# Order of VectorE's work within a slot, and the share of dense groups per slot, in an infini-attention and gated-GLU kernel

## The chip, the cores and the metric

The kernel runs on one core of a Trainium2 chip. The time is the device time of one execution in microseconds; the profile's span runs from the first to the last instruction of the program within it. Five engines work side by side, each through its own queue in order: TensorE (PE; its weight loads are PEld), VectorE (DVE), ScalarE (ACT), GpSimd (POOL) and SyncE (SP), which here issues most DMAs.

## What is computed

Part A is a layer norm, three projections, and attention in 32 heads of 20 over 4 segments of 512 rows: causal softmax attention inside a segment, and a read of a memory `M`, `z` that the earlier segments left, mixed by a gate per head. Part B is a gated GLU on the same normalised input, 640 to 1536 and back. The result is `x + A * silu(B)`.

```python
xn = _layernorm(x)                                   # [1, 2048, 640], bf16
for s in range(4):                                   # segments
    p = softmax(q_s @ k_s.T * scale + causal)        # per head
    a_dot = p @ v_s
    a_mem = (phi(q_s) @ M) / (phi(q_s) @ z + 1e-6)   # phi(t) = t + 1 if t > 0 else exp(t)
    o = g * a_mem + (1 - g) * a_dot
    M, z = M + phi(k_s).T @ v_s, z + phi(k_s).sum()
out = x + (o @ wo) * silu((sigmoid(xn @ w_gate) * (xn @ w_up)) @ w_down)
```

## The kernel before

**Slots.** The main loop (L666 to L717) goes through 4 segments of 20 slots. A slot handles one unit of a pair of head groups: `scores` (L495) multiplies keys by queries for four heads into `Sps`, one PSUM tile of four banks, ScalarE takes the exponential of all of it into `pt` (L506), and GpSimd zeroes what lies above the diagonal (L509). One slot later `weigh` (L513) multiplies `pt` by the values into `Aps` (L526), one PSUM tile with a single buffer. Five units make a pair; after the units 2 and 4 of a pair the accumulated `Aps` of a head group is complete, and VectorE does the division (L532 to L535: reciprocal, gate, product into `od`). As units are weighed one slot later, divisions fall into slots 3 and 5, 8 and 10, 13 and 15, 18 and 20 of a segment's count, and the slot after each begins a new `Aps` tile.

**What fills a slot.** Beside scores and weighting there are two kinds of work. The dense groups of the GLU wait in a list, `bulk`: `gate` (L408, matmuls into `gp`, tanh `tg` on ScalarE), `up` (L418, matmuls into `up`, then VectorE's gating product `hT`, L426) and `down` (L429, twelve matmuls into `yp`, tanh `t` on ScalarE, VectorE's product `aa`, L440). Everything else stands in a heap, `tasks`, with a due time in slots and a cost in us of TensorE time (L620 to L656): projections of the next segment (`k_chunk`, `q_chunk`, `v_tile`: `psk`, `psq`, `psv`), the bound `q_bound` (`cps`), the memory's update (`dm`) and read (`am`), the output projection (`o_proj`: `sp`), and work without matmuls: layer-norm statistics (`ln_stats`, L217 to L219) and normalisation (`ln_norm`, L234), the features (`phi`, L347: minimum and sum on VectorE, exponential of `mn` on ScalarE at L355, maximum on VectorE at L359), reductions (`k_max`), and the DMAs that store, relay and transpose. A task may put a follow-up into the heap with `later`.

**How a slot is filled.** `fill` (L682) runs tasks that are due, and dense groups as long as a budget is owed, first up to 0.45 of the slot with 45% of the budget, then, after `weigh`, up to its end. The budget is worked out anew in each slot, so that slots rich in other work get fewer dense groups; and while dense groups are left, each slot gets more until `FLOOR` = 1.2 is reached (L712). Each engine's instructions stand in its queue in just the order in which these functions issue them (`manual_schedule`, L95).

**PSUM.** Of eight banks `Sps` has four, `Aps` one, and all other matmuls share three buffers of the pool `ps_d`, tag `d`. A buffer is free again when ScalarE or VectorE has read it; the pool hands out one that is free in its own plan.

**Start.** `startup` (L552) does segment 0's projections and the relays of queries and keys through DRAM (`Qs`, `Ks`, `Cs` into `QT`, `KT`), loads the GLU's weights in pieces (`load_glu`), normalises segment 1 and runs the first seven dense groups. SP issues its DMAs in the order of the code: `load_glu(1, 0)` (L593) stands ahead of `c_in(0, (0,))` (L594), which loads `QT` from `Cs`.

Of the kernel before, what the change touches and what calls it, by code (L numbers as in the profile page):

```python
# [53 lines left out]
FLOOR = 1.2  # L54
# [5 lines left out]
def kernel(  # L60
# [168 lines left out]
    def ln_norm(n, p, i):  # L229
# [8 lines left out]
        if n == 0:  # L238
            pT = ps_d.tile([P, DC, P], BF, name="pT", tag="d")
# [23 lines left out]
    def k_chunk(n, c):  # L263
# [4 lines left out]
        ps = ps_d.tile([P, L], F32, name="psk", tag="d")  # L268
# [26 lines left out]
    def q_chunk(n, c):  # L295
# [4 lines left out]
        ps = ps_d.tile([P, L], F32, name="psq", tag="d")  # L300
# [9 lines left out]
    def q_bound(n):  # L310
        s = st[n]
        ps = ps_d.tile([P, L], F32, name="cps", tag="d")
# [24 lines left out]
    def v_tile(n, j, half):  # L337
        s = st[n]
        ps = ps_d.tile([P, HB], F32, name="psv", tag="d")
# [27 lines left out]
    def m_update(n, cs):  # L367
        s = st[n]
        dm = ps_d.tile([P, len(cs), HW * VW], F32, name="dm", tag="d")
# [17 lines left out]
    def mem_read(n, j, b):  # L387
# [3 lines left out]
        am = ps_d.tile([P, 16, VW], F32, name="am", tag="d")  # L391
# [16 lines left out]
    def gate(n, f):  # L408
        s = st[n]
        gp = ps_d.tile([P, L], F32, name="gp", tag="d")  # L410
# [7 lines left out]
    def up(n, f):  # L418
        s = st[n]
        ps = ps_d.tile([P, L], F32, name="up", tag="d")  # L420
# [5 lines left out]
        nc.vector.scalar_tensor_tensor(out=h[:], in0=s["tg"][:], scalar=1.0, in1=ps[:], op0=ALU.add, op1=ALU.mult)  # L426
        s.setdefault("hT", []).append(h)

    def down(n, j, half):  # L429
        s = st[n]  # L430
        if half == 0:
            s[f"aa{j}"] = fpool.tile([P, D], BF, name="aa", bufs=4)
        hs = slice(half * HB, (half + 1) * HB)
        yp = ps_d.tile([P, HB], F32, name="yp", tag="d")
        for f in range(FC):
# [4 lines left out]
        nc.vector.scalar_tensor_tensor(out=s[f"aa{j}"][:, hs], in0=t2[:], scalar=1.0, in1=yp[:],  # L440
                                       op0=ALU.add, op1=ALU.mult)
# [18 lines left out]
    def o_last(n):  # L460
        po = ps_d.tile([P, 4, P], BF, name="po", tag="d")
# [12 lines left out]
    def o_proj(n, j, half):  # L474
# [4 lines left out]
        sp = ps_d.tile([P, HB], F32, name="sp", tag="d")  # L479
# [67 lines left out]
    def warm(count):  # L547
        ps = ps_d.tile([P, L], F32, name="wps", tag="d")
# [3 lines left out]
    def startup():  # L552
# [24 lines left out]
        for c in range(DC):  # L577
# [15 lines left out]
        load_glu(1, 0)  # L593
# [10 lines left out]
        take(1)  # L604
        ln_norm(1, 1, 0)
        take(1)
        ln_norm(1, 1, 1)
        take(2)
# [49 lines left out]
    def run_task():  # L658
        time, _, cost, fn, a = heapq.heappop(tasks)
        clock[0] = max(clock[0], time)  # L660
        fn(*a)
        return cost

    owed = 0.0
    due, held = [], []
    for n in range(NSEG):  # L666
# [4 lines left out]
        keep = 4 if n >= NSEG - 2 else 0  # L671
# [95 lines left out]
```

## Time and profile before

| | |
|---|---|
| median of 3 runs | 353.14 us (349.23, 353.14, 353.32) |
| profiled execution | 352.11 us, its span 350.3 us |
| mean granted clock of TensorE | 0.987 |
| first score matmul (slot 0) | 34.0 us |
| last slot begins (slot 79) | 330.9 us |
| TensorE, VectorE, ScalarE, GpSimd busy | 330.3, 216.0, 234.2, 110.7 us |

How to read the profile's lines: `L436 PE MATMUL yp<-Wd,hT 128*128 128x320 bf16 x384` is line 436 of the kernel, engine, operation, what it writes and reads, shapes and count. In a timeline a line begins with its start and its length in us, and merges equal instructions that follow each other; what stands in brackets is the idle time of that engine just before, and what ended it. In the list of waits the numbers are us in total, times, and the longest. In the table by stage each engine has its busy time and its instructions; behind them stand the granted clock, the share of DMA and GB/s. A matmul's record is longer than the distance to the next one, since matmuls are pipelined.

### The profile page before, as it was taken

The page shows a single profiled execution, that of the slowest core. Times are in us where ns is not written, and L with a number is a line of the kernel's source. Part 1 is how long each engine was busy: PE and PEld are TensorE (multiplying, and loading weights), DVE is VectorE, ACT ScalarE, POOL GpSimd, SP SyncE. Part 2 cuts the span into 40 slices and gives each one's busy share as a digit, 9 for nine tenths or more (in the row PEclk, how much of TensorE's full clock was granted, in tenths as well). Part 3 has the DMA queues.
Part 4 walks back from the last instruction along what each step waited for, and adds up shares of the span by engine and source line. Part 5 has one row for each costly group of instructions (what it writes and reads, how often), then busy time and mean ns, then how long its engine had stood idle before and what let it go on. Part 6 is the DMA issues. An engine that isn't in the chain of part 4 may idle for free.

```text
span 350.3 us, 8363 instructions
## 1 busy us (share of the span) xinstructions
PE 330.3 (94%) x3359; PEld 188.9 (54%) x3402; DVE 216.0 (62%) x541; ACT 234.2 (67%) x258; POOL 110.7 (32%) x157
## 2 busy tenths in 40 slices
PE   8998899998969999999987999999999999999995
PEld 7543355545645466554554446555446755544673
DVE  5364374468975456669759556766585688533445
ACT  3652689868694677657777566666778877776730
POOL 6644223222153222323225132231323323223214
PEclk9999999999998999999999899999999999999998
DMA  7947775564721621034740261104231341210032
GB/s 226 353 162 225 140 198 113 177 196 115 193 76 22 112 77 39 19 103 103 176 127 17 52 110 49 37 34 137 84 97 42 39 113 40 75 40 2 2 60 75
DMA packets 54725, 35.53 MB, mean 101 GB/s; under 512 B 28576, under 2 KB 54688, under 8 KB 54688
## 3 DMA queue, kind: packets, MB, share of 16 engines
q1 hardware_dynamic: 52480, 32.23, 35.5%
q10 hardware_dynamic: 2208, 2.79, 2.5%
q8 instruction: 26, 0.43, 0.5%
q14 instruction: 11, 0.09, 0.1%
HBM read 20.19 MB, written 8.39 MB: 82 GB/s over the span
## 4 chain that ended last, share of the span: by engine, by line
PE 73%; DVE 9%; ACT 8%; DMA 4%; issue 3%; SPq 1%; POOL 0%; ACTq 0%; DVEq 0%; POOLq 0%
PE gp L413 13%; PE up L423 13%; PE yp L436 10%; PE Aps L526 8%; PE sp L481 6%; PE Sps L501 5%; PE psv L341 5%; PE psk L270 5%; ACT pt L506 5%; PE psq L302 5%; DMA pkt<-k 2%; PE wps L550 2%; DMA xnT<-xn 1%; PE am L395 1%; ACT mn L355 1%
## 5 line engine op out<-in xcount | busy, mean ns | idle before, releaser
L506 ACT ACTIVATE pt<-Sps 128x2048 bf16<-128x2048 f32 x80 | 150.2, 1877 | 26.4 <-PE Sps L501 22.2
L509 POOL TENSOR_SCALAR_AFFINE_SELECT pt<-pt 128x1024 bf16<-128x1024 bf16 (+1 forms) x80 | 75.9, 948 | 210.2 <-ACT pt L506 210.2
L423 PE MATMUL up<-xnT,Wu 128*128 128x512 bf16 x230 | 59.1, 379 | 2.3 <-DVE hT L426 1.5
L436 PE MATMUL yp<-Wd,hT 128*128 128x320 bf16 x384 | 60.0, 309 | 0.0
L413 PE MATMUL gp<-xnT,Wg 128*128 128x512 bf16 x219 | 58.0, 379 | 1.4 <-issue 0.3
L526 PEld LDWEIGHTS <-pt 128*128 128x128 bf16 x1280 | 42.9, 96 | 22.7 <-DVE od L535 11.5
L426 DVE SCALAR_TENSOR_TENSOR hT<-tg,up 128x512 bf16<-128x512 bf16 x48 | 32.7, 682 | 32.7 <-PE up L423 30.3
L526 PE MATMUL Aps<-va,pt 128*128 128x21 bf16 x1280 | 44.8, 173 | 8.5 <-DVE od L535 7.2
L416 ACT ACTIVATE tg<-gp 128x512 bf16<-128x512 f32 x48 | 28.6, 597 | 26.7 <-PE gp L413 21.1
L436 PEld LDWEIGHTS <-hT 128*128 128x128 bf16 x384 | 36.3, 100 | 16.5 <-issue 2.6
L440 DVE SCALAR_TENSOR_TENSOR aa<-t,yp 128x320 bf16<-128x320 bf16 x32 | 15.6, 487 | 30.7 <-ACT t L439 30.6
L501 PE MATMUL Sps<-QT,KT 24*128 24x128 bf16 (+3 forms) x512 | 32.6, 302 | 1.4 <-DMA QT<-Cs 1.1
L423 PEld LDWEIGHTS <-Wu 128*128 128x128 bf16 x240 | 20.5, 97 | 24.9 <-issue 6.1
L413 PEld LDWEIGHTS <-Wg 128*128 128x128 bf16 x240 | 20.8, 97 | 23.7 <-issue 4.3
L439 ACT ACTIVATE t<-yp 128x320 bf16<-128x320 f32 x32 | 13.9, 436 | 19.9 <-PE yp L436 19.9
L341 PE MATMUL psv<-Wv,xnT 128*128 128x320 bf16 x160 | 26.5, 299 | 0.2
L481 PE MATMUL sp<-Wo,oT 128*128 128x320 bf16 x160 | 25.9, 299 | 0.0
L483 DVE SCALAR_TENSOR_TENSOR aa<-aa,sp 128x320 bf16<-128x320 bf16 x32 | 15.5, 486 | 16.1 <-PE sp L481 16.1
L270 PE MATMUL psk<-xnT,Wk 128*128 128x512 bf16 x95 | 23.8, 380 | 0.2
L302 PE MATMUL psq<-xnT,Wq 128*128 128x512 bf16 x93 | 23.5, 379 | 0.4 <-issue 0.2
L355 ACT ACTIVATE mn<-mn 128x512 bf16<-128x512 bf16 x30 | 19.0, 632 | 5.9 <-DVE mn L351 5.9
L501 PEld LDWEIGHTS <-KT 24*128 24x128 bf16 x512 | 9.5, 92 | 24.0 <-issue 22.6
(73 smaller groups left out, 328.6 us busy)
## 6 DMA issues: line engine op xcount, KB each, us to landing
KT<-Ks SPq DMA_DIRECT2D x32, 80.0 KB
QT<-Qs SPq DMA_DIRECT2D x32, 80.0 KB
xr<-in_A_x_dram SPq DMA_DIRECT2D x15, 160.0 KB
out_dram<-xr SPq DMA_DIRECT2D x15, 160.0 KB
xt<-in_A_x_dram SPq DMA_DIRECT2D x6, 320.0 KB
Wg<-in_B_w_gate_dram SPq DMA_DIRECT2D x3, 640.0 KB
Wu<-in_B_w_up_dram SPq DMA_DIRECT2D x3, 640.0 KB
Wd<-in_B_w_down_dram ACTq DMA_DIRECT2D x1, 1920.0 KB
```

Of the source, the lines that this page charges most:

```text
L270: nc.tensor.matmul(ps[:], lhsT=W["k"][:, k, c * P:(c + 1) * P], rhs=s["xnT"][:, k, :], start=(k == 0), stop=(k == DC - 1))
L302: nc.tensor.matmul(ps[:], lhsT=W["q"][:, k, c * P:(c + 1) * P], rhs=s["xnT"][:, k, :], start=(k == 0), stop=(k == DC - 1))
L341: nc.tensor.matmul(ps[:], lhsT=s["xnT"][:, k, j * P:(j + 1) * P], rhs=W["v"][:, k, half * HB:(half + 1) * HB], start=(k == 0), stop=(k == ...
L413: nc.tensor.matmul(gp[:], lhsT=Wg[f // 4][:, k, fo:fo + P], rhs=s["xnT"][:, k, :], start=(k == 0), stop=(k == DC - 1))
L423: nc.tensor.matmul(ps[:], lhsT=Wu[f // 4][:, k, fo:fo + P], rhs=s["xnT"][:, k, :], start=(k == 0), stop=(k == DC - 1))
L426: nc.vector.scalar_tensor_tensor(out=h[:], in0=s["tg"][:], scalar=1.0, in1=ps[:], op0=ALU.add, op1=ALU.mult)
L436: nc.tensor.matmul(yp[:], lhsT=s["hT"][f][:, j * P:(j + 1) * P], rhs=W["d"][:, f, hs], start=(f == 0), stop=(f == FC - 1))
L481: nc.tensor.matmul(sp[:], lhsT=s["oT"][:, j, c, :], rhs=W["o"][:, c, hs], start=(c == 0), stop=(c == DC - 1))
L501: nc.tensor.matmul(Sps[:, r, c0:c0 + ncol], lhsT=kt[32 * r:32 * r + KR, gi, kb * P:(kb + 1) * P], rhs=qt[32 * r:32 * r + KR, gi, kb * P:L] ...
L506: nc.scalar.activation(pt[:], Sps[:], ACT.Exp, scale=SCALE)
L509: nc.gpsimd.affine_select(out=diag, in_=diag, compare_op=ALU.is_ge, fill=0.0, base=0, pattern=[[0, 4], [0, cnt], [1, P]], channel_multipli ...
L526: nc.tensor.matmul(A[:, qb, r, :], lhsT=pt[:, r, off:off + P], rhs=V[4 * (n % 2) + kb][:, 4 * g + r, :], start=first, stop=True, skip_grou ...
```

## The change

Five things are changed.

1. Tasks with a cost of at most 0.1 (statistics, normalisation, features, reductions, follow-ups, DMAs) go into a second heap, `soft`. The first half of a slot runs only `tasks`, the second half both, in order of due time.
2. VectorE's products of `up` and `down` are put off when they come up in a slot's first half: `empty` keeps them in `pending` until `weigh` has issued its matmuls and the division, or until the third next tile of the pool is taken (`dtile`). `down` puts out all but the last before it goes on.
3. The dense groups' share is worked out once per segment (`level`, `fixed`); a running sum `given` is compared with a running `goal`, of which 45% of a slot's share comes ahead of `weigh`. `FLOOR` is gone.
4. In the startup `load_glu(1, 0)` moves up behind the first store of `Qs`, and the normalisations of segment 1's last two row blocks move out of the startup, into the heap with due times 1.67 and 1.92.
5. `run_task` sets the clock that follow-ups count from to the task's own due time; at the end `drain` empties both heaps.

All tiles of the pool `ps_d` are taken through `dtile`; of these replacements one is shown.

```diff
@@ -51,7 +51,7 @@
 NU = len(UNITS)
 NSLOT = NG // 2 * NU
 WARM = 40
-FLOOR = 1.2
+FIRST = 0.45
 PASS = [0.41, 0.41, 0.41, 0.2, 0.61]
 R = NSLOT / 24
 
@@ -95,13 +95,32 @@
     ctx.enter_context(tc.manual_schedule(engines={ENG.PE, ENG.Activation, ENG.DVE, ENG.Pool, ENG.SP}))
 
 
-    tasks = []
+    tasks, soft = [], []
     count = [0]
     clock = [0.0]
+    pending = []
 
     def at(time, cost, fn, *a):
         count[0] += 1
-        heapq.heappush(tasks, (time, count[0], cost, fn, a))
+        heapq.heappush(tasks if cost > 0.1 else soft, (time, count[0], cost, fn, a))
+
+    seq = [0]
+    delay = [False]
+
+    def flush(keep=0):
+        while len(pending) > keep:
+            pending.pop(0)[1]()
+
+    def dtile(shape, dtype, name):
+        seq[0] += 1
+        while pending and pending[0][0] <= seq[0] - 3:
+            pending.pop(0)[1]()
+        return ps_d.tile(shape, dtype, name=name, tag="d")
+
+    def empty(fn):
+        pending.append((seq[0], fn))
+        if not delay[0]:
+            flush()
 
     def later(lag, fn, *a):
         at(clock[0] + lag * R, 0.0, fn, *a)
@@ -236,7 +255,7 @@
         j = 2 * p + i
         dst = s["xnT"][:, :, j * P:(j + 1) * P]
         if n == 0:
-            pT = ps_d.tile([P, DC, P], BF, name="pT", tag="d")
+            pT = dtile([P, DC, P], BF, "pT")
             for c in range(DC):
                 nc.tensor.transpose(pT[:, c, :], xn[:, c * P:(c + 1) * P], ident[:])
             nc.scalar.copy(dst, pT[:])
...
@@ -417,28 +436,34 @@
 
     def up(n, f):
         s = st[n]
-        ps = ps_d.tile([P, L], F32, name="up", tag="d")
+        ps = dtile([P, L], F32, "up")
         fo = (f % 4) * P
         for k in range(DC):
             nc.tensor.matmul(ps[:], lhsT=Wu[f // 4][:, k, fo:fo + P], rhs=s["xnT"][:, k, :],
                              start=(k == 0), stop=(k == DC - 1))
         h = gpool.tile([P, L], BF, name="hT", bufs=FC)
-        nc.vector.scalar_tensor_tensor(out=h[:], in0=s["tg"][:], scalar=1.0, in1=ps[:], op0=ALU.add, op1=ALU.mult)
+        tg = s["tg"]
+        empty(lambda: nc.vector.scalar_tensor_tensor(out=h[:], in0=tg[:], scalar=1.0, in1=ps[:],
+                                                     op0=ALU.add, op1=ALU.mult))
         s.setdefault("hT", []).append(h)
 
     def down(n, j, half):
         s = st[n]
         if half == 0:
             s[f"aa{j}"] = fpool.tile([P, D], BF, name="aa", bufs=4)
+            if j == 0:
+                flush()
         hs = slice(half * HB, (half + 1) * HB)
-        yp = ps_d.tile([P, HB], F32, name="yp", tag="d")
+        flush(1)
+        yp = dtile([P, HB], F32, "yp")
         for f in range(FC):
             nc.tensor.matmul(yp[:], lhsT=s["hT"][f][:, j * P:(j + 1) * P], rhs=W["d"][:, f, hs],
                              start=(f == 0), stop=(f == FC - 1))
         t2 = fpool.tile([P, HB], BF, name="t2")
         nc.scalar.activation(t2[:], yp[:], ACT.Tanh, scale=0.25)
-        nc.vector.scalar_tensor_tensor(out=s[f"aa{j}"][:, hs], in0=t2[:], scalar=1.0, in1=yp[:],
-                                       op0=ALU.add, op1=ALU.mult)
+        aa = s[f"aa{j}"]
+        empty(lambda: nc.vector.scalar_tensor_tensor(out=aa[:, hs], in0=t2[:], scalar=1.0, in1=yp[:],
+                                                     op0=ALU.add, op1=ALU.mult))
 
 
     def o_add(n, j, c0, c1):
...
@@ -581,6 +606,7 @@
                 relay(0, 0, Ks, KT)
             elif c == 2:
                 stage_out(0, 0, Qs, QT, "q5")
+                load_glu(1, 0)
             if c < 2:
                 ln_stats(1, 0, c, c + 1)
         make_bd()
@@ -590,7 +616,6 @@
         relay(0, 0, Qs, QT)
         q_bound(0)
         stage_out(0, 1, Qs, QT, "q5")
-        load_glu(1, 0)
         c_in(0, (0,))
         load_glu(1, 1)
         ln_stats(1, 1, 0, 1)
@@ -601,11 +626,9 @@
         ln_norm(1, 0, 1)
         take(1)
         ln_stats(1, 1, 1, 2)
-        take(1)
-        ln_norm(1, 1, 0)
-        take(1)
-        ln_norm(1, 1, 1)
-        take(2)
+        take(4)
+        at(R * 2.0, 0.0, ln_norm, 1, 1, 0)
+        at(R * 2.3, 0.0, ln_norm, 1, 1, 1)
         load_glu(2, 0)
         load_glu(2, 1)
         relay(0, 1, Ks, KT)
@@ -655,13 +678,17 @@
         at(NSLOT * NSEG - 8 + 0.5 * j, 0.0, xr_load, NSEG - 1, j)
         at(NSLOT * NSEG - 0.9 + 0.2 * j, 0.0, o_ready, NSEG - 1, j, DC - 1)
 
-    def run_task():
-        time, _, cost, fn, a = heapq.heappop(tasks)
-        clock[0] = max(clock[0], time)
+    def run_task(heap):
+        time, _, cost, fn, a = heapq.heappop(heap)
+        clock[0] = time
         fn(*a)
         return cost
 
-    owed = 0.0
+    def drain():
+        flush()
+        while tasks or soft:
+            run_task(min((h for h in (tasks, soft) if h), key=lambda h: h[0][:2]))
+
     due, held = [], []
     for n in range(NSEG):
         st[n]["od"] = opool.tile([P, 4, D], BF, name="od")
@@ -669,51 +696,47 @@
             bulk += [(1.09, fn, (n, f)) for f in range(FC) for fn in (gate, up)]
         bulk += [(1.64, down, (n, j, h)) for j in range(4) for h in range(2)]
         keep = 4 if n >= NSEG - 2 else 0
+
+        left = sum(b[0] for b in bulk[:len(bulk) - keep])
+        fixed = [PASS[i % NU] + sum(t[2] for t in tasks if i <= t[0] - NSLOT * n < i + 1) for i in range(NSLOT)]
+        level = min(fixed)
+        while sum(max(level - f, 0.0) for f in fixed) < left:
+            level += 0.01
+        given, goal = 0.0, 0.0
+
+        def fill(until, heaps):
+            nonlocal given
+            while True:
+                ready = [h for h in heaps if h and h[0][0] < until]
+                if ready:
+                    run_task(min(ready, key=lambda h: h[0][:2]))
+                if len(bulk) > keep and given + 0.5 * bulk[0][0] <= goal:
+                    cost, fn, a = bulk.pop(0)
+                    given += cost
+                    fn(*a)
+                elif not ready:
+                    break
+
         for slot in range(NSLOT):
             pair, u = divmod(slot, NU)
             now = NSLOT * n + slot
-
-            def more():
-                nonlocal owed
-                cost, fn, a = bulk.pop(0)
-                owed -= cost
-                fn(*a)
-
-            def fill(until, share):
-                nonlocal owed
-                owed += budget * share
-                while True:
-                    if tasks and tasks[0][0] < until:
-                        owed -= run_task()
-                        if not (len(bulk) > keep and owed >= 0.5 * bulk[0][0]):
-                            continue
-                    if len(bulk) > keep and owed >= 0.5 * bulk[0][0]:
-                        more()
-                    elif not (tasks and tasks[0][0] < until):
-                        break
-
-            left = sum(b[0] for b in bulk[:max(len(bulk) - keep, 0)])
-            fixed = [PASS[i % NU] + sum(t[2] for t in tasks if now + i - slot <= t[0] < now + i - slot + 1)
-                     for i in range(slot, NSLOT)]
-            level = min(fixed)
-            while sum(max(level - f, 0.0) for f in fixed) < left:
-                level += 0.01
-            budget = max(level, fixed[0])
-            owed = -PASS[u]
+            share = max(level - fixed[slot], 0.0)
             pt = scores(n, pair, u)
-            fill(now + 0.45, 0.45)
+            delay[0] = True
+            goal += FIRST * share
+            fill(now + 0.45, (tasks,))
             for w in due:
                 weigh(*w)
+            delay[0] = False
+            flush()
             due, held = held, []
             due.append((n, pair, u, UNITS[u][0][0], pt))
             if u == 2:
                 held.append((n, pair, u, 1, pt))
-            fill(now + 1.0, 0.55)
-            while len(bulk) > keep and budget - owed - PASS[u] < FLOOR:
-                more()
+            goal += (1.0 - FIRST) * share
+            fill(now + 1.0, (tasks, soft))
         while len(bulk) > keep:
             cost, fn, a = bulk.pop(0)
-            owed -= cost
             fn(*a)
 
 
@@ -721,8 +744,7 @@
     fn(*a)
     for w in due:
         weigh(*w)
-    while tasks:
-        run_task()
+    drain()
     n = NSEG - 1
     for j in range(4):
         o_add(n, j, (DC - 1) * P, D)
@@ -733,8 +755,7 @@
     for j in range(4):
         for h in range(2):
             o_proj(n, j, h)
-            while tasks:
-                run_task()
+            drain()
 
 # ---- launch: one core; inputs and outputs as the reference has them ----
 _INS = ['A_x', 'A_wq', 'A_wk', 'A_wv', 'A_wo', 'A_beta', 'B_x', 'B_w_gate', 'B_w_up', 'B_w_down']
```

More of the change, by code (lines that the diff above doesn't have):

```diff
@@ L311, in q_bound @@
         s = st[n]
-        ps = ps_d.tile([P, L], F32, name="cps", tag="d")
+        ps = dtile([P, L], F32, "cps")
         for c in range(DC):
@@ L338, in v_tile @@
         s = st[n]
-        ps = ps_d.tile([P, HB], F32, name="psv", tag="d")
+        ps = dtile([P, HB], F32, "psv")
         for k in range(DC):
@@ L409, in gate @@
         s = st[n]
-        gp = ps_d.tile([P, L], F32, name="gp", tag="d")
+        gp = dtile([P, L], F32, "gp")
         fo = (f % 4) * P
@@ L460, in o_last @@
     def o_last(n):
-        po = ps_d.tile([P, 4, P], BF, name="po", tag="d")
+        po = dtile([P, 4, P], BF, "po")
         for j in range(4):
@@ L547, in warm @@
     def warm(count):
-        ps = ps_d.tile([P, L], F32, name="wps", tag="d")
+        ps = dtile([P, L], F32, "wps")
         for i in range(count):
```

10 lines of the change are left out of this document (5 added, 5 removed).

## The prediction

> **What bounds it now.** I read the page first, then the list of waits, the table by stage and the timeline around each stage that stood out. A slot is one pass of the main loop; it begins with its score matmuls (L501, `Sps`). There are 80 slots, 20 to a segment, numbered 0 to 79.
>
> ```profile
> PE 330.3 (94%) x3359; PEld 188.9 (54%) x3402; DVE 216.0 (62%) x541; ACT 234.2 (67%) x258; POOL 110.7 (32%) x157
> PE 73%; DVE 9%; ACT 8%; DMA 4%; issue 3%; SPq 1%; POOL 0%; ACTq 0%; DVEq 0%; POOLq 0%
> ...
> PE Aps L526 <- DVE od L535: 7.2, 6, 2.2
> ACT mn L355 <- DVE mn L351: 5.9, 6, 1.9
> ...
> 100.00:120.00 20.00, 17.23 (x174) 9.02 (x173) 10.95 (x30) 13.37 (x15) 8.20 (x14) 0.91 0.30 54
> 180.00:200.00 20.00, 17.68 (x179) 10.36 (x178) 12.91 (x37) 13.30 (x18) 7.64 (x13) 0.91 0.18 43
> ```
>
> TensorE is busy 94% of the span and 73% of the chain that ended last, so what counts is where it stands still. The list of waits names one repeated cause: the weighting matmuls (L526) wait for VectorE's division (L535), because the single buffer `Aps` is free only when the division has read it: 7.2 us in 6 waits. The two stages with a granted clock of 0.91 hold the ends of segments 0 and 1.
>
> ```profile
> 96.77 0.40 PE L501 MATMUL Sps<-QT,KT 24*128 24x256 bf16 x8
> 101.00 1.79 PE L436 MATMUL yp<-Wd,hT 128*128 128x320 bf16 x12
> 102.83 0.40 PE L501 MATMUL Sps<-QT,KT 24*128 24x128 bf16 x8
> 105.16 0.76 PE L526 MATMUL Aps<-va,pt 128*128 128x21 bf16 x24 [1.93 <-DVE od L535]
> 105.78 3.24 PE L436 MATMUL yp<-Wd,hT 128*128 128x320 bf16 x12
> 108.95 0.57 PE L501 MATMUL Sps<-QT,KT 24*128 24x512 bf16 x4
> ...
> 188.65 0.40 PE L501 MATMUL Sps<-QT,KT 24*128 24x128 bf16 x8
> 191.20 0.81 PE L526 MATMUL Aps<-va,pt 128*128 128x21 bf16 x24 [2.16 <-DVE od L535]
> 191.85 3.16 PE L436 MATMUL yp<-Wd,hT 128*128 128x320 bf16 x12
> 194.95 0.39 PE L501 MATMUL Sps<-QT,KT 24*128 24x512 bf16 x4
> ```
>
> In slot 19 (102.83) and slot 39 (188.65) the division comes late and TensorE idles 1.93 and 2.16 us; right after it twelve `yp` matmuls take 3.24 and 3.16 us where the same twelve took 1.79 before: the clock fell to half. So one late division costs about 2 us plus 1.4 us of clock.
>
> Prices of TensorE's work, from first start to last end less the last one's tail:
>
> ```profile
> 36.26 1.24 PE L413 MATMUL gp<-xnT,Wg 128*128 128x512 bf16 x5
> 40.40 0.56 PE L526 MATMUL Aps<-va,pt 128*128 128x21 bf16 x16
> 44.88 0.84 PE L341 MATMUL psv<-Wv,xnT 128*128 128x320 bf16 x5
> ```
>
> A gate or up group of five takes 1.08 us ((1.24-0.38)/4 a matmul, times five), a `down` group of twelve 1.63, a `psv` group 0.68, sixteen `Aps` 0.41, 24 of them 0.6; scores about 0.35. With these, slots 17 to 19 hold 7.2 us of work and last 12.2 (96.77 to 108.95): 5.0 us lost. Slot 39 holds 2.6 and lasts 6.3: 3.7 lost. Most other slots last what their work sums to.
>
> **The change, part by part.** It takes away no instruction. TensorE, ScalarE and GpSimd issue the same work; what moves is order.
>
> *Start.*
>
> ```profile
> 27.63 0.50 SPq L144 DMA_DIRECT2D Wg<-in_B_w_gate_dram  x1
> 29.68 1.29 SPq L334 DMA_DIRECT2D QT<-Cs  x4
> 34.04 1.19 PE L501 MATMUL Sps<-QT,KT 24*128 24x512 bf16 x4 [1.12 <-DMA QT<-Cs]
> ...
> 37.55 1.12 DVE L234 TENSOR_SCALAR xn<-xt,mv,rstd 128x640 bf16<-128x640 bf16 x2 [6.54 <-DMA xnT<-xn]
> 39.32 1.24 PE L423 MATMUL up<-xnT,Wu 128*128 128x512 bf16 x4 [1.49 <-DVE hT L426]
> ```
>
> Slot 0 waits 1.12 us for `QT<-Cs`, and its four score matmuls take 1.19 us instead of 0.40. These loads (29.68) stand on SP's queue right behind `Wg` (27.63, 640 KB). The change issues that `Wg` after the first `Qs` store, some 5 us sooner, so those bytes no longer stand ahead of `QT<-Cs`. In slot 1 VectorE holds at two normalisations (L234, 6.54 us, for a transpose to land); the gating product behind them keeps a PSUM buffer, and TensorE idles 1.49 us. The two normalisations move behind slot 1's product. On SP their transposes now stand behind the last `Wg` and `Wu` and the relays; the first `psv` group that reads them comes in slot 5, 10 us later. At stake: 1.12+0.79+1.49 = 3.4. Bounds 0 and 3.4; I take **-3.0**, as each wait's cause is moved out of its way.
>
> *Divisions in the middle of a segment.*
>
> ```profile
> 87.68 0.77 PE L526 MATMUL Aps<-va,pt 128*128 128x21 bf16 x24 [1.06 <-DVE od L535]
> 178.50 0.57 PE L526 MATMUL Aps<-va,pt 128*128 128x21 bf16 x16 [1.06 <-DVE od L535]
> 258.95 0.57 PE L526 MATMUL Aps<-va,pt 128*128 128x21 bf16 x16 [0.68 <-DVE od L535]
> 268.73 0.76 PE L526 MATMUL Aps<-va,pt 128*128 128x21 bf16 x24 [0.34 <-DVE od L535]
> ```
>
> These are slots 14, 36, 56 and 59. In front of each division stood feature, norm or gating work; now at most two evacuations do. After the weighting TensorE has at least 1.1 us of other work before it needs `Aps` again, about what the division takes (0.25+0.17+0.49, below). So 1.06 (slot 14), 0.68 and 0.34 (56, 59) go: **-1.1** and **-1.0**. What is late next: in slot 13 a feature's exponential behind an `up` product delays the next `pt`, in slots 5 and 6 there is less dense work than ScalarE has; I put **+0.5** there and **+0.4** in slots 43, 57 and 58, about half of one such wait of before (5.9 us in 6); bounds 0 and 2.
>
> *The new wait: exponentials of features before `pt`.* ScalarE and VectorE work their queues in order. Feature work now all lies in the second half of a slot, behind the `down` product.
>
> ```profile
> 177.31 0.63 ACT L355 ACTIVATE mn<-mn 128x512 bf16<-128x512 bf16 x1 [1.85 <-DVE mn L351]
> 177.46 0.25 DVE L532 RECIPROCAL rd<-Aps 128x16 f32<-128x16 f32 x1
> 177.75 0.17 DVE L533 TENSOR_TENSOR rd<-rd,omg 128x16 f32<-128x16 f32 x1
> 177.96 0.49 DVE L535 TENSOR_TENSOR od<-Aps,rd 128x320 bf16<-128x320 f32 x1
> 177.85 1.86 ACT L506 ACTIVATE pt<-Sps 128x2048 bf16<-128x2048 f32 x1
> ...
> 96.93 0.44 ACT L439 ACTIVATE t<-yp 128x320 bf16<-128x320 f32 x1
> 97.40 0.49 DVE L440 SCALAR_TENSOR_TENSOR aa<-t,yp 128x320 bf16<-128x320 bf16 x1 [0.92 <-ACT t L439]
> 98.26 0.48 DVE L217 BATCH_NORM_STATS2 bs<-xt 128x6 f32<-128x320 bf16 x1
> 99.17 0.21 DVE L219 BATCH_NORM_AGGREGATE mv<-bs 128x2 f32<-128x12 f32 x1
> 99.30 0.24 DVE L351 TENSOR_SCALAR mn<-q 128x512 bf16<-128x512 bf16 x1
> ```
>
> Slot 36 of before shows the pattern: ScalarE sat idle 1.85 us for a minimum (L351), and `pt` (177.85) came only behind that exponential. In the new order of slot 15 (and 35) stand: last `yp`, its tanh, its `aa` product, the minimum, the exponential (L355), then slot 16's `pt`. Steps from the rows: tanh 0.16 (96.77 to 96.93) and 0.44, product 0.03 and 0.49, minimum 0.3, exponential 0.1 and 0.54 to the next start (177.31 to 177.85), `pt` 1.86: slot 17's scores come 3.9 us after slot 16 began. In slot 17 (and 37) two statistics and an aggregate lie between as well (98.26 to 99.30, 1.05 us): slot 18 lasts 5.0 us.
>
> Slot 16 of after holds scores, `cps` and sixteen `Aps`, 1.1 us: 2.8 lost. Slot 18 holds 3.9: 1.1 lost. Slot 19 loses 0.3. I expect the clock to fall after 2.8 us idle, 8 chances in 10, at 1.45 (3.24-1.79): 1.2. Sum 5.4, where 5.0 are lost now: **+0.4** for this stage; the late division is gone, the late `pt` has its place.
>
> Segment 1: slot 36 keeps its `down` group, 2.7 us of work in 3.9: 1.2 lost, for 1.06 before. Slot 38 loses 1.1. Slot 39 has a `down` group ahead of its weighting and loses nothing: -3.7. With 2 chances in 10 of a half clock after 36 or 38 (0.3): **-2.2**. Bounds for both stages together: -9 (no exponential comes last) to +4 (four idle stretches, each with half clock). Segment 2's last slots have no statistics and an `up` in place of `yp` in slot 55, with the minimum ahead of it: little lost.
>
> *Dense groups.* `FLOOR` goes and each slot's share is fixed for the segment: the last groups of a segment come later (slot 39 gets two `down` groups instead of one, slot 18 two). The sum of work is the same; it pays only where a wait is filled, counted above. In segment 3 an `up` of slot 66 waits for a buffer and slot 77 is shorter than one `pt`: **+0.4**, nearest rows 0.34 and 0.68.
>
> *What else moves.* Stores, relays and transposes of the features are issued half a slot later on SP, the loads of `Wd` and `Wo` on ScalarE's queue too. Their readers come a slot or more later (`QT` of slot 20 is issued in slot 17), so I cost them at nothing; if that cover is gone, each is a wait like the 1.12 of slot 0.
>
> *Clock rule.* The idle stretches of 1.93 and 2.16 us were followed by half clock, the one of 1.49 was not. The Trainium skill, page "TensorE: Matmul & The Clock Gate", section "HAM oscillation — how this bites in real kernels", gives as the rule no idle gaps over about 3.4 us; by it slot 16 would cost no clock and the sum would be 1.2 us less. The measurement decides: gaps of 2 us tripped it here.
>
> **Sum.** -3.0 -1.1 -1.0 +0.5 +0.4 +0.4 -2.2 +0.4 = -5.6. The profiled execution took 352.11 us (span 350.3) and stands 1.0 under the median of the runs shown, 353.14. So 346.5, which is 1.9% under that median.
>
> **Rivals.**
>
> ```profile
> L426 DVE SCALAR_TENSOR_TENSOR hT<-tg,up 128x512 bf16<-128x512 bf16 x48 | 32.7, 682 | 32.7 <-PE up L423 30.3
> L355 ACT ACTIVATE mn<-mn 128x512 bf16<-128x512 bf16 x30 | 19.0, 632 | 5.9 <-DVE mn L351 5.9
> ```
>
> (A) The above, 346.5; its own range 342 to 350. Chance 0.48.
>
> (B) The exponentials do not come last, because VectorE and ScalarE run ahead of TensorE more than the rows let me count. Then 2.8+1.1+0.3+1.2 and 1.2+1.1+0.3 are not lost either: 338.5 us. For it: only 5.9 us of such waits (6) in before. Against it: the chain starts at TensorE's own `yp`, so running ahead does not shorten it. Chance 0.18.
>
> (C) Held buffers. A product held until after the division keeps one of three PSUM buffers. Where three short groups follow at once (slots 26 and 46: `up`, `psv`, `am`, then `gp`), strict rotation would make `gp` wait for VectorE's read of `am` (about 0.9) and the product (0.68), less 0.4 of `Aps`: 1.2 each, and the like in slot 43, 3.6: 350.1. Against it: in the new program's order `gp` takes the buffer that `psv` left. The Trainium skill says, on its page "PSUM — Partial Sum Buffer", section "Summary: rules for kernel authors", "Evacuate promptly"; that speaks against holding. No row of before shows such a hold. Chance 0.14.
>
> (D) Slower. Features now lie behind products in every slot that has one, 30 exponentials (L355), and each may hold the next `pt`. At 0.6 us each, a third of slot 36's wait, that is 18 us, of which 6 are counted: 358.5, slower. It decides from 0.4 us each on (5.6 gained and 6 counted, over 30). For it: ScalarE is in order and `pt` the longest instruction. Against: in slots of 4 us of dense work `pt` has 2 us to spare. Chance 0.12.
>
> (E) Nothing comes of it: the start stays bound by the loads and the segment ends trade one wait for another: 352. Chance 0.08.
>
> **Numbers.** Forecast 346.5. Leaving out half of B below and most of D above gives 339 to 355. Over 2% means under 346.1 or over 360.2 against the median, about what a measurement of this kernel can tell from no change (its runs lie from 349.23 to 353.32). Something under half of A and all of B: faster 0.40. The rest of A, C, E and a third of D: 0.52. Slower 0.08.
>
> **What would show it.** Right: no wait of `Aps` for `od` over 0.5 us in slots 14, 19, 39; slot 0's scores without a wait for `QT<-Cs`; slot 16 near 3.9 us, with ScalarE idle for the minimum L351. Wrong: `Aps` still late in 19 or 39; slot 16 under 3 us (B); waits of `gp` or `psv` for `hT` (C); `pt` late in slots 10 to 14 and 30 to 34 (D).

## The result and the profile after

The changed kernel takes 348.70 us (median of 20 runs, 346.44 to 350.90), the kernel before 353.34 us (20 runs, 349.23 to 356.79): a ratio of 0.9897, interval 0.9865 to 0.9930. All ratios are of fast runs alone, here without five runs of the kernel before that took over 1.5% more than its fastest, so this one lies nearer to 1 than the quotient of the medians (0.9869). The kernel is 1.0% faster; forecast were 346.5 us and 1.9%. The profiled execution took 350.39 us (span 348.3 for 350.3 before). It is one of the longer ones: runs of the changed kernel whose mean granted clock was 1.00 took 346.44 to 346.66 us, those at 0.987 to 0.990 348.77 to 350.90; those between, at 0.992 to 0.995, took 346.69 to 349.81, so the clock accounts for only a part of the spread.

First the page's busy times and chain, then TensorE's own rows of the list of waits (total, times, longest):

```profile
PE 333.0 (96%) x3402; PEld 187.4 (54%) x3402; DVE 215.1 (62%) x541; ACT 233.8 (67%) x258; POOL 111.0 (32%) x157
PE 79%; DVE 7%; ACT 6%; DMA 5%; issue 2%; SPq 0%; ACTq 0%; DVEq 0%
```

```profile
PE Sps L526 <- ACT pt L531: 4.9, 4, 2.4
PE Sps L526 <- DMA QT<-Cs: 1.7, 2, 1.2
...
PE psk L289 <- ACT k L291: 1.0, 1, 1.0
PE psv L360 <- ACT tg L435: 0.5, 1, 0.5
PE gp L432 <- DVE hT L446: 0.4, 1, 0.4
PE yp L460 <- DVE hT L446: 0.4, 1, 0.4
...
PE Aps L551 <- DVE od L560: 0.2, 1, 0.2
```

On the chain that ended last VectorE's share has fallen from 9% to 7%, ScalarE's from 8% to 6%. The 7.2 us of waits for the division have become 0.2. In their place stand 4.9 us in four waits of the scores for `pt`. The timeline shows where; the chain that the prediction wrote down for slot 16 (92.63) is there piece by piece:

```profile
92.63 0.40 PE L526 MATMUL Sps<-QT,KT 24*128 24x128 bf16 x8
92.80 0.44 ACT L463 ACTIVATE t<-yp 128x320 bf16<-128x320 f32 x1 [0.88 <-PE yp L460]
93.27 0.49 DVE L465 SCALAR_TENSOR_TENSOR aa<-t,yp 128x320 bf16<-128x320 bf16 x1 [0.64 <-ACT t L463]
93.67 0.28 DVE L370 TENSOR_SCALAR mn<-q 128x512 bf16<-128x512 bf16 x1
94.05 0.63 ACT L374 ACTIVATE mn<-mn 128x512 bf16<-128x512 bf16 x1 [0.82 <-DVE mn L370]
94.59 1.86 ACT L531 ACTIVATE pt<-Sps 128x2048 bf16<-128x2048 f32 x1
96.50 0.40 PE L526 MATMUL Sps<-QT,KT 24*128 24x256 bf16 x8 [2.43 <-ACT pt L531]
...
102.09 0.40 PE L526 MATMUL Sps<-QT,KT 24*128 24x512 bf16 x4
106.94 0.40 PE L526 MATMUL Sps<-QT,KT 24*128 24x128 bf16 x8 [0.89 <-ACT pt L531]
107.55 0.76 PE L551 MATMUL Aps<-va,pt 128*128 128x21 bf16 x24 [0.20 <-DVE od L560]
```

`pt` could have started at 93.2, behind the tanh, since its scores were there; ScalarE instead waited 0.82 us for VectorE's minimum, which stood behind `aa`, and then ran that feature's exponential. The late division at slot 19 (1.93 us) is now 0.20.

The table by stage (the granted clock stands behind POOL's busy time), and TensorE at the start:

```profile
36.00:40.00 4.00, 4.00 (x19) 1.19 (x17) 0.69 (x1) 2.13 (x2) 0.68 (x1) 0.57 1.24 223
98.00:102.00 4.00, 4.00 (x33) 2.44 (x31) 0.93 (x2) 1.65 (x2) 1.10 (x1) 0.59 0.40 114
180.00:200.00 20.00, 19.17 (x209) 11.63 (x206) 15.22 (x42) 15.06 (x19) 8.37 (x14) 1.00 0.21 47
```

```profile
33.97 0.37 PE L526 MATMUL Sps<-QT,KT 24*128 24x512 bf16 x1 [1.16 <-DMA QT<-Cs]
34.89 0.95 PE L526 MATMUL Sps<-QT,KT 24*128 24x512 bf16 x3 [0.55 <-DMA QT<-Cs]
...
37.24 2.34 PE L432 MATMUL gp<-xnT,Wg 128*128 128x512 bf16 x5
```

The half clock of 192 us is gone (1.00), that of 106 us has moved to 98, and there is a new one behind slot 0's wait, which did not go: the `gp` group at 37.24 takes 2.34 us instead of 1.24.

### The profile page after: what moved, and what is told of

It is laid out like the page before. It is cut to its first block, busy times and chain, and to the rows that moved or that the text cites. A ratio compares the mean times of both kernels' runs of the same rounds, so it can differ in the third digit from the quotient of the medians.

```text
span 348.3 us, 8395 instructions
## 1 busy us (share of the span) xinstructions
PE 333.0 (96%) x3402; PEld 187.4 (54%) x3402; DVE 215.1 (62%) x541; ACT 233.8 (67%) x258; POOL 111.0 (32%) x157
## 4 chain that ended last, share of the span: by engine, by line
PE 79%; DVE 7%; ACT 6%; DMA 5%; issue 2%; SPq 0%; ACTq 0%; DVEq 0%
PE gp L432 13%; PE up L442 13%; PE yp L460 13%; PE Aps L551 8%; PE Sps L526 7%; PE psq L321 6%; PE sp L506 6%; PE psk L289 6%; PE psv L360 5%; ACT pt L531 3%; DMA pkt<-k 2%; DMA Cs<-cb 1%; PE dm L392 1%; PE am L414 1%; DMA Qs<-q 1%
## 5 line engine op out<-in xcount | busy, mean ns | idle before, releaser
L432 PE MATMUL gp<-xnT,Wg 128*128 128x512 bf16 x240 | 60.7, 384 | 0.5 <-DVE hT L446 0.4
L442 PE MATMUL up<-xnT,Wu 128*128 128x512 bf16 x240 | 60.1, 381 | 0.0
L460 PE MATMUL yp<-Wd,hT 128*128 128x320 bf16 x384 | 58.7, 304 | 0.4 <-DVE hT L446 0.4
L442 PEld LDWEIGHTS <-Wu 128*128 128x128 bf16 x240 | 21.2, 97 | 22.9 <-issue 2.3
L321 PE MATMUL psq<-xnT,Wq 128*128 128x512 bf16 x100 | 24.3, 380 | 0.0
```

Source lines behind the costliest of these rows:

```text
L321: nc.tensor.matmul(ps[:], lhsT=W["q"][:, k, c * P:(c + 1) * P], rhs=s["xnT"][:, k, :], start=(k == 0), stop=(k == DC - 1))
L432: nc.tensor.matmul(gp[:], lhsT=Wg[f // 4][:, k, fo:fo + P], rhs=s["xnT"][:, k, :], start=(k == 0), stop=(k == DC - 1))
L442: nc.tensor.matmul(ps[:], lhsT=Wu[f // 4][:, k, fo:fo + P], rhs=s["xnT"][:, k, :], start=(k == 0), stop=(k == DC - 1))
L460: nc.tensor.matmul(yp[:], lhsT=s["hT"][f][:, j * P:(j + 1) * P], rhs=W["d"][:, f, hs], start=(f == 0), stop=(f == FC - 1))
```

## The experiments

Each ratio is to the kernel before on the same chip, with its interval. The runs are numbered in the order in which they ran; the expectations refer to each other by it.

| run | kernel | median, us | ratio |
|---|---|---|---|
| | changed kernel | 348.70 | 0.9897 (0.9865 to 0.9930) |
| 1 | before, with the startup (point 4) alone | 350.21 | 0.9983 (0.9942 to 1.0023) |
| 2 | changed, Wg behind QT<-Cs | 347.69 | 0.9887 (0.9835 to 0.9938) |
| 3 | changed, exponentials behind `pt` | 343.85 | 0.9774 (0.9711 to 0.9836) |
| 4 | changed, keys' features early | 348.30 | 0.9911 (0.9877 to 0.9944) |
| 5 | changed, no product put off | 348.79 | 0.9887 (0.9844 to 0.9931) |
| 6 | changed, one heap | 345.75 | 0.9791 (0.9747 to 0.9834) |
| 7 | changed, without points 1 and 2 | 345.86 | 0.9801 (0.9756 to 0.9846) |
| 8 | changed, Wg before the KT relay | 349.10 | 0.9882 (0.9829 to 0.9935) |
| 9 | run 3, only `aa` put off | 342.01 | 0.9689 (0.9647 to 0.9732) |
| 10 | run 9 and four more edits | 341.44 | 0.9695 (0.9657 to 0.9732) |
| 11 | run 10, Cs ahead of the QT relay | 338.19 | 0.9607 (0.9551 to 0.9664) |
| 12 | changed, Cs ahead of the QT relay | 347.19 | 0.9852 (0.9789 to 0.9914) |

**The late `pt` (run 3).** On the changed kernel, an exponential that comes up in segments 1 to 3 is kept, and issued right behind the next slot's `pt` (at most two features are under way, so that two buffers `mn` do):

```diff
+        def put():
+            exps.append((clock[0], exp))
...
-        later(0.8, exp)
+        later(0.8, put if n else exp)
...
             pt = scores(n, pair, u)
+            put_out()
```

> The changed kernel, where the exponential of a feature (segments 1 to 3) is always issued behind the next slot's pt. Theory T: at the ends of segments 0 and 1 the late pt comes from the chain tanh, aa, minimum, exponential ahead of it. Slot 16 falls from 3.9 to about 2.4 us (one pt and its scores), slot 36 from 3.8 to 2.9, slots 18 and 38 from 4.8 to 3.9, and no half clock follows slot 16: 4.5 to 6 us less than the changed kernel, ratio 0.977 to 0.973. Rival U: pt is late there because ScalarE and VectorE have more work than TensorE, whatever its order; slots 16 and 18 gain under 0.5 us each, ratio 0.988.

```profile
92.08 0.40 PE L540 MATMUL Sps<-QT,KT 24*128 24x128 bf16 x8
92.59 1.88 ACT L545 ACTIVATE pt<-Sps 128x2048 bf16<-128x2048 f32 x1
94.37 0.62 ACT L384 ACTIVATE mn<-mn 128x512 bf16<-128x512 bf16 x1
94.52 0.40 PE L540 MATMUL Sps<-QT,KT 24*128 24x256 bf16 x8 [1.01 <-ACT pt L545]
...
98.63 0.40 PE L540 MATMUL Sps<-QT,KT 24*128 24x512 bf16 x4
102.52 0.40 PE L540 MATMUL Sps<-QT,KT 24*128 24x128 bf16 x8
```

Slot 16 lasts 2.44 us, slot 18 3.89, and the ratio falls by 1.2 points, from 0.9897 to 0.9774, with intervals that do not touch. Theory T holds, Rival U falls: the order on ScalarE's queue made `pt` late, not the amount of work. The 1.01 us that are left are one `pt` in a slot of 1.1 us of work.

**Which part pays (runs 5 to 7).** Three kernels take points 1 and 2 out of the changed kernel, singly and together:

```diff
-            delay[0] = True
+            delay[0] = False
```

```diff
-            fill(now + 0.45, (tasks,))
+            fill(now + 0.45, (tasks, soft))
```

> The changed kernel without point 2: no product is put off, the second heap stays. Theory S: the second heap alone takes the late divisions away; slots 14 and 39 stay without a wait for the division, and the short waits for a held product go (hT in slots 35, 43 and 66, 0.4 to 0.7 us each): ratio to before 0.986 to 0.989. Theory H: the holding does it; with aa and hT ahead of the division again, the weighting of slots 14, 19 and 39 waits about 1 us each: 0.993 to 0.997.

> The changed kernel, where the first half of a slot runs both heaps; the products stay put off. Theory S: statistics and features stand ahead of the divisions again, slot 14 loses 1.1 us, slots 19 and 39 about 2 us each and half a clock more, in return slot 16's pt is less late: ratio 0.995 to 1.0. Theory H: the divisions stay on time: 0.988 to 0.991.

> The changed kernel without points 1 and 2 (both heaps in the first half, no product put off); the dense share per segment and the startup stay. Theory S: as the run before it, 0.995 to 1.0: the share moves work but takes no late division away. Rival G: the gain of the segment ends (3.3 us in slots 36 to 39) comes from slot 39's two down groups, so most of it stays: 0.989 to 0.992.

TensorE's waits, first without put-off products, then with one heap:

```profile
PE Sps L526 <- ACT pt L531: 4.9, 4, 2.4
...
PE Aps L551 <- DVE od L560: 1.4, 1, 1.4
```

```profile
PE Sps L526 <- ACT pt L531: 1.3, 1, 1.3
...
PE Aps L551 <- DVE od L560: 0.9, 1, 0.9
```

And one wait and the timeline with neither, where the kernel before lost 1.06 (slot 14), 1.93 (slot 19) and 2.16 us (slot 39):

```profile
PE Aps L551 <- DVE od L560: 2.4, 2, 2.0
```

```profile
81.27 0.35 PE L551 MATMUL Aps<-va,pt 128*128 128x21 bf16 x8
81.48 1.79 PE L460 MATMUL yp<-Wd,hT 128*128 128x320 bf16 x12
...
84.62 0.75 PE L551 MATMUL Aps<-va,pt 128*128 128x21 bf16 x24
...
103.82 0.76 PE L551 MATMUL Aps<-va,pt 128*128 128x21 bf16 x24 [2.00 <-DVE od L560]
...
183.21 1.80 PE L460 MATMUL yp<-Wd,hT 128*128 128x320 bf16 x12
185.38 0.76 PE L551 MATMUL Aps<-va,pt 128*128 128x21 bf16 x24 [0.37 <-DVE od L560]
```

Theory S, that the second heap makes the gain, falls: it put both kernels with one heap at 0.995 to 1.0, and they came out at 0.9791 and 0.9801, better than any theory had them. Without points 1 and 2 the kernel is at 0.9801, and with the startup alone (below) at 0.9983, so the share (with point 5, which came along) brings about 1.8%; this is the difference of two runs, and no run has the share alone.

In slot 13 it moved the `down` group from ahead of the weighting to behind it (81.48 behind 81.27); the product `aa`, which waits for a tanh behind `pt`, so left the place ahead of the division. In slot 39 it put a `down` group ahead of the weighting (183.21), and that covers the same late division: 0.37 us of wait. The waits of slots 36, 56 and 59 are gone as well. Only slot 19, which has no group there, still waits, 2.00 us.

The second heap shortens that wait (2.0 to 1.4 us, and 0.9 to 0.2 with products put off) and makes `pt` late in four places instead (4.9 us of wait, against 1.3 in one). With products put off the ratio is 0.9897 with it and 0.9791 without, and the intervals do not touch; with none put off it is 0.9887 and 0.9801, and the intervals just overlap (0.9844 and 0.9846). Whether the second heap pays once the exponentials stand behind `pt`, as in runs 3 and 9 to 11, was not tried.

Putting products off is neutral (0.9897 and 0.9887 with two heaps, 0.9791 and 0.9801 with one): in the changed kernel it spares 1.2 us at slot 19's division (1.4 to 0.2) and costs the waits of `yp`, `psv` and `gp`, 0.4, 0.5 and 0.4 us.

**The start (runs 1, 2, 8, 4, then 11 and 12).** Point 4 on the kernel before; then on the changed kernel the load of Wg later, sooner, and the keys' features sooner:

```diff
             elif c == 2:
                 stage_out(0, 0, Qs, QT, "q5")
+                load_glu(1, 0)
...
-        ln_norm(1, 1, 0)
...
+        at(R * 2.0, 0.0, ln_norm, 1, 1, 0)
```

> The kernel before with point 4 of the change alone (Wg of the startup issued behind the first Qs store, the last two normalisations due in slots 1 and 2). Theory T: the 640 KB of Wg are moved, not removed; they now stand ahead of the Cs store and of QT<-Qs instead of ahead of QT<-Cs, so the scores of slot 0 still wait 1.1 us or more for QT<-Cs. Only the 1.49 us for hT in slot 1 go: 0.996 of before, with the first slots 1.2 to 1.5 us shorter; a half clock behind slot 0's wait would take that back (1.0). Rival R, as the prediction had it: both waits go, 3.0 us, 0.991.

```diff
                 stage_out(0, 0, Qs, QT, "q5")
-                load_glu(1, 0)
...
         c_in(0, (0,))
+        load_glu(1, 0)
         load_glu(1, 1)
```

> The changed kernel with that load of Wg issued behind the first QT<-Cs instead. Theory T: QT<-Cs is issued at 30 us or sooner and has landed when slot 0 begins; its waits of 1.16, 0.55 and 0.2 us go, and the half clock of slots 0 and 1 with them: 2 us under the changed kernel without the clock, 4 with it; ratio to before 0.984 to 0.978. Rival: the loads as a whole are the bound, and the same bytes are missed by the first gate that reads Wg's second piece (slot 1 or 2): ratio as the changed kernel, 0.990.

```diff
                 stage_out(0, 1, Ks, KT, "k5")
+                load_glu(1, 0)
                 relay(0, 0, Ks, KT)
...
-                load_glu(1, 0)
```

> The changed kernel with the startup's load of Wg issued one step sooner, behind the second Ks store and ahead of the KT relay. Theory T: the DMA engines are idle there (share 0.60 from 18 to 20 us, 0.14 from 20 to 22 us), so the 640 KB pass while the Ks and Qs stores are still to come; QT<-Cs is issued by 30 us, the waits of slot 0 (1.16, 0.55 us) fall under 0.3 us, and nothing else waits: 1.5 us under the changed kernel, ratio 0.984 to 0.986. Rival L: the load delays the relay of KT and with it Qs, QT and Cs by as much: 0.990 and the same wait in slot 0.

```diff
-                    at(R * (2.6 + 0.8 * c), 0.0, phi, 0, "k5", c)
+                    at(R * (1.6 + 0.8 * c), 0.0, phi, 0, "k5", c)
```

> The changed kernel with the features of segment 0's keys due 0.83 slots earlier. Theory T: slot 8 loses 1.0 us because the cast into k waits for the transposes pkt<-k, which the second heap issues half a slot later than before; that wait goes, 1.0 us less than the changed kernel, ratio 0.987. Rival: the transposes are bound by SP's queue (five of them 8.9 us behind the loads of the startup), so an earlier due time only lengthens their wait in the queue: 0.990 and the same wait in slot 8.

Waits of the startup alone, then of Wg behind:

```profile
PE psv L341 <- DMA xnT<-xn: 1.3, 1, 1.3
...
PE Sps L501 <- DMA QT<-Cs: 0.6, 2, 0.3
```

```profile
PE up L442 <- DMA Wu<-in_B_w_up_dram: 1.0, 1, 1.0
...
PE gp L432 <- DMA Wg<-in_B_w_gate_dram: 0.6, 1, 0.6
...
PE Sps L526 <- DMA QT<-Cs: 0.3, 1, 0.3
```

With the startup alone the 1.49 us for `hT` go, slot 0 still waits 0.6 us (at least 1.1 by Theory T, nothing by Rival R), and 1.3 us come back in slot 5, where `psv` waits for the transposes that point 4 put behind the relays; its ratio does not differ from 1. With Wg behind, slot 0 waits 0.3 us, but the gates and `up` wait for their weights, 1.6 us, as the rival had it.

With Wg sooner the wait in slot 0 stayed (1.27 and 0.38 us), against Theory T. This wait differs much from profile to profile even where the startup is the same (0.9 to 2.2 us in the changed kernel and runs 3 to 7 and 9), so one profile tells only large differences of it. The keys' features sooner took the wait of `psk` away, 1.0 us; the 0.6 us for `xnT` in that profile are not its doing, as run 5 has them too (1.1 us). The ratio does not tell it from the changed kernel.

So Wg's place only shifts the wait. What stays in all these kernels is the order on SP's queue, here of run 10, where the load of Wg was issued at 19.10 and the DMA engines moved nothing from 27 to 28 us (start, length):

```profile
22.55 0.39 SPq L316 DMA_DIRECT2D Qs<-q  x1
27.12 1.43 SPq L280 DMA_DIRECT2D QT<-Qs  x4
28.65 0.35 SPq L351 DMA_DIRECT2D Cs<-cb  x1
31.67 1.27 SPq L359 DMA_DIRECT2D QT<-Cs  x4
```

```profile
25.36 0.58 ACT L343 CAST cb<-cps 128x512 bf16<-128x512 f32 x1
```

`cb` is ready at 25.94, but its store stands behind the relay of QT, which waits on SP for the Qs store to land: 2.7 us later. The step behind it differs too: from the store of Cs to the issue of its load pass 4.4 us in the changed kernel (27.68 to 32.03), 2.9 in the kernel before (26.76 to 29.68), 2.8 with Wg behind (28.08 to 30.85), but 3.9 with Wg sooner (28.31 to 32.18), so what lengthens it stays open. The last two kernels move the store ahead:

```diff
-        relay(0, 0, Qs, QT)
         q_bound(0)
+        relay(0, 0, Qs, QT)
```

> The kernel of the run before, with q_bound and its Cs store ahead of the relay QT<-Qs on SP's queue. Theory Q: slot 0's wait is no matter of bytes but of SP's order: cb is ready at 25.9 us, its store is issued at 28.7 because the relay ahead of it waits for the Qs store to land (27.1), and QT<-Cs 3.0 us later. With the store ahead, Cs goes out at 26 us, QT<-Cs at 29 to 30, and slot 0 waits less than 0.2 us; without that wait no half clock follows: 1 us less than the run before by the wait and 1.5 to 2 us more by the clock, ratio to before 0.961 to 0.966. Rival B, bytes: the DMA engines need their time for Wg, Qs and Cs in any order, and slot 0 waits 0.8 us or more: 0.968 to 0.971.

> The changed kernel with that one edit (q_bound ahead of the relay QT<-Qs). Theory Q: slot 0's waits of 1.16 and 0.55 us fall under 0.3 us and the half clock of slots 0 and 1 goes; the rest stays: ratio 0.983 to 0.986. Rival B: here the 640 KB of Wg are in flight when Cs goes out (store to landing 4.3 us instead of 3.0), so that at least 0.8 us of wait stay: 0.988 to 0.990.

Theory Q holds for slot 0: in both runs the list has no wait for QT<-Cs any more, and the granted clock of the first slots is 1.00. In the profiled executions most of it came back at once as waits for `xnT` and `Wu` (1.8 and 0.9 us in run 11, 1.5 and 1.1 in run 12); that of run 11, 340.74 us, is 2.5 us above its median, so its other runs need not have them. Over the runs the step brought 0.9% to run 10 and 0.5% to the changed kernel, with intervals that overlap.

**Both causes mended (runs 9 and 10).** Exponentials behind `pt`, and only the products of `down` put off:

```diff
-    def empty(fn):
+    def empty(fn, hold=True):
         pending.append((seq[0], fn))
-        if not delay[0]:
+        if not (delay[0] and hold):
...
-        empty(lambda: nc.vector.scalar_tensor_tensor(out=h[:], in0=tg[:], scalar=1.0, in1=ps[:],
-                                                     op0=ALU.add, op1=ALU.mult))
+        empty(lambda: nc.vector.scalar_tensor_tensor(out=h[:], in0=tg[:], scalar=1.0, in1=ps[:],
+                                                     op0=ALU.add, op1=ALU.mult), False)
```

> The changed kernel with the exponentials of segments 1 to 3 behind the next pt (as in the third run), and only the products of down put off; those of up stand where TensorE's group does. Theory T2: the second heap is kept for its divisions, its late pt is gone, and the waits for a held product go too (yp in slot 35 0.2 us, psv in slot 43 0.5, gp in slot 66 0.4): 1.0 to 1.5 us under the third run, ratio to before 0.973 to 0.975. Rival V: products of up ahead of the division delay it; slots 14, 19 or 39 wait 0.5 us or more for od, and the ratio is that of the third run, 0.977, or more.

The waits of `yp`, `psv` and `gp` went and no wait for a division is over 0.3 us: T2 holds, Rival V falls; the ratio came out better than either had it. Then four more edits, two of them in the startup (Wg as in run 8, and `c_in(0, (0,))` ahead of the second Qs store):

```diff
-            at(w + R * 19.2, 1.12, q_bound, m)
+            at(w + R * 19.2, 0.28, q_bound, m)
...
-    at(6.8, 0, load_late, "d", B_w_down)
+    at(8.2, 0, load_late, "d", B_w_down)
```

> The kernel of the run before with four more edits: the cost of q_bound in the plan is 0.28 instead of 1.12 (its five cps matmuls take 0.28 us), so that slot 16 gets a down group; the load of Wd is due at 8.2 slots instead of 6.8; the startup's Wg goes behind the second Ks store; QT<-Cs ahead of the second Qs store. Theory T2: slot 16 loses 0.3 instead of 1.4 us, slot 14 (2.1 us of work, shorter than one pt) 0.3; slot 8 loses nothing, as the 1.9 MB of Wd no longer stand ahead of the last transpose pkt<-k; slot 0 waits under 0.3 us: 2.5 to 3.5 us under the run before, ratio 0.965 to 0.968. Rival: the transposes are slow by themselves and slot 8 keeps its 1.0 us, and QT<-Cs is held by the chain Qs, QT, Cs on SP's queue: 0.970 to 0.972.

Its waits have no row for `psk`, and the wait for `pt` fell from 1.0 to 0.3 us; slot 0 still waited 1.1 us. So Theory T2 holds in slots 8, 14 and 16, and not in slot 0. The ratio, 0.9695, does not differ from the kernel ahead of it (0.9689): what the profiles gain, 2.8 us of span, 1.2 of them by a shorter wait in slot 0, is less than these runs can tell. With `q_bound` ahead of the relay as well, 338.19 us, this is the fastest kernel here: 0.9607, interval 0.9551 to 0.9664.

## Why the prediction was right, and where not

The time lay inside the range, and about half of the gain forecast came. One part of the 1.9% was in no step: the sum of -5.6 us is 1.6% of the profiled execution, and the rest is that this execution stood 1.0 us under the median. That the time came out within the range is in part luck, as terms that failed stand beside terms that came out better. Step by step, in the two profiled executions:

| step | forecast | measured |
|---|---|---|
| slots 16, 18, 36, 38 last | 3.9, 5.0, 3.9, 5.0 us | 3.87, 4.85, 3.80, 4.79 us |
| slot 14 | -1.1 | -1.2 (4.99 to 3.76) |
| slots 16 to 19 | +0.4 | +0.2 (15.38 to 17.25, with 1.63 us more work) |
| slots 36 to 39 | -2.2 | -3.3 (18.67 to 17.00, with 1.63 us more work) |
| slots 0 and 1 | -3.0 | +0.75 (7.94 to 9.77, with an `up` of 1.08 us more) |
| slots 56 and 59 | -1.0 | -1.0 (neither wait is left) |
| slots 5, 6, 13, 43, 57, 58, 66, 77 | +1.3 | waits of 0.1 (slot 14's scores, for `pt`), 0.5 (slot 43) and 0.4 (slot 66) |
| slot 8 | 0 | +1.0 |

**Right.** The new wait, down to the order of its pieces; that slot 16's idle time would be followed by half clock (it was, in this execution); that slot 39's `down` group ahead of the weighting would end its loss.

**Wrong: the start.** "I take -3.0, as each wait's cause is moved out of its way." Of the two causes only the product behind the normalisations was moved out; for `QT<-Cs` the queue was read for bytes and not for the wait at its head. The Cs store stood behind a relay that waits, and moving the 640 KB left that as it was. A half clock came on top: in run 7, which has the same startup and no half clock there, slots 0 and 1 take 7.96 us, so that without it, and less the `up` of 1.08, the term would be -1.1. In the profiled execution it is 3.75 us off, as much as all that lies between the sum (-5.6) and the two spans (-2.0); the other misses cancel. (By the medians 4.6 us came; the profiled execution of the changed kernel is a long one.)

**Wrong: transposes costed at nothing.** "Their readers come a slot or more later": the cast into `k` does not read what the transposes `pkt<-k` write, but it overwrites what they still read. ScalarE's cast in the kernel before, then in the changed kernel:

```profile
64.18 0.58 ACT L272 CAST k<-psk 128x512 bf16<-128x512 f32 x1 [1.31 <-DMA pkt<-k]
```

```profile
64.96 0.59 ACT L291 CAST k<-psk 128x512 bf16<-128x512 f32 x1 [2.45 <-DMA pkt<-k]
```

So the cast waited before as well, and TensorE did not. There, one group (`up`) stood between the `psk` of slot 7 and that of slot 8, which could take the third buffer; now two do (`gp`, `up`), and the `psk` of slot 8 needs the buffer that the cast has yet to read, 1.0 us. With one heap the wait stays (1.0 and 0.9 us in runs 6 and 7), and in the kernel before, the changed kernel and run 7 alike the last transpose is issued 5.7 us ahead of slot 8. So the wait does not come from the second heap's half slot, as run 4's Theory T had it. By this order it comes from the share; no run moved that one group by itself. The wait was gone with the features due sooner (run 4), and in run 10, where the load of Wd came later, but where slot 7 also had one group less.

**Right sum, wrong shares.** "In front of each division stood feature, norm or gating work; now at most two evacuations do" describes the new order of a slot, and it was not what paid: the waits of slots 14, 36, 56 and 59 went with one heap as well. "The sum of work is the same; it pays only where a wait is filled" undersold the share: it is the part that pays, by what it puts ahead of a weighting and what it takes away from there. The second heap, the first point of the change, cost about 1% in the kernel as it is.

**Rivals.** (B) fell: the exponentials come last. (C)'s hold is there, 0.4, 0.5 and 0.4 us and not 3.6; putting off only `aa` ended it. (D)'s mechanism is real at four slots, 4.9 us, not at all thirty. (E) has its half in the start, which brought nothing.

## What to carry to other kernels

Work that is moved behind one engine's deadline lands ahead of another's: before moving VectorE's work behind the division, look at which ScalarE instruction waits for it, and what stands behind that on ScalarE's queue. A late evacuation is cured as well by independent matmuls in front of its reader as by an earlier evacuation, so try the order of the dense work first. When a DMA is late, look at what waits at the head of its issuing queue, and not at the bytes ahead of it alone.

## What the runs showed of the clock

The same idle stretch does not always cost clock. The longest wait for `pt`, 2.4 us in slot 16, stands in six of these profiles (the changed kernel and runs 2, 4, 5, 8 and 12). It was followed by half clock in the changed kernel (0.59 above) and in runs 4, 5 and 8, and not in runs 2 and 12. Of run 2 the stage that holds its end (slot 17 begins at 95.28) shows

```profile
94.00:98.00 4.00, 2.71 (x39) 1.97 (x39) 0.56 (x2) 4.00 (x5) 1.10 (x1) 1.00 0.57 159
```

It is the same at the start. In ten of the profiles the small score matmuls of slot 0 waited 0.9 us or more in all. Half clock followed in six of them (the changed kernel and runs 3, 6, 8, 9 and 10), and not in the kernel before and in runs 4, 5 and 7. The shortest of these waits (run 3, 0.72 and 0.20 us) had it, and one of the longest (run 5, 1.90 and 0.22 us) had not. The wait and the clock behind it, first of run 3, then of run 5:

```profile
33.67 0.37 PE L540 MATMUL Sps<-QT,KT 24*128 24x512 bf16 x1 [0.72 <-DMA QT<-Cs]
```

```profile
36.00:38.00 2.00, 2.00 (x7) 0.73 (x5) 0.69 (x1) 1.40 (x1) 0.53 (x1) 0.51 1.74 308
```

```profile
34.80 0.37 PE L526 MATMUL Sps<-QT,KT 24*128 24x512 bf16 x1 [1.90 <-DMA QT<-Cs]
```

```profile
36.00:38.00 2.00, 2.00 (x9) 0.84 (x10) 0.36 (x1) 1.61 (x1) 0.00 (x0) 1.00 1.08 333
```

The rule of the Trainium skill, page "TensorE: Matmul & The Clock Gate", section "HAM oscillation — how this bites in real kernels", that gaps over about 3.4 us re-throttle TensorE, does not cover these: no gap here is that long, the longest being 2.4 us. So the length of the stretch alone does not decide. What does stays open; no run varied it by itself.
